# TransNormer attention and a squared-ReLU MLP: neighbouring tokens in a tile, one output transfer for two tiles, and a new order in the opening

## The chip, the cores and the metric

The kernel runs on one core of one Trainium2 chip. The metric is the device time of a launch in microseconds. A core has a matrix engine (TensorE, PE in the profile; its weight loads are PEld), three engines for elementwise work (VectorE or DVE, ScalarE or ACT, GpSimd or POOL) and SyncE (SP), which here only issues transfers. Sixteen DMA engines move the data.

## The reference

The inputs are `q`, `k`, `v` of (8 batches, 8 heads, 576 tokens, 64 features), and two weights that arrive as float64.

```
kv  = einsum('bhsd,bhse->bhde', k, v)
out = einsum('bhsd,bhde->bhse', q, kv)
x   = out / sqrt(mean(out*out, -1) + 1e-6) * g_norm      # per head
x   -> (4608 tokens, 512)
y   = (relu(x @ w_in) ** 2) @ w_out                      # 512 -> 2048 -> 512
```

## The kernel before

**Tiles and strips.** A batch has 576 tokens: four tiles of 128 (`C = 4`) and a rest of 64. The rests of two batches make one tile, so two batches give nine tiles (`PAIR = 9`) and there are 36. Four tiles are a strip of 512 tokens (`NT = 4`), and the main loop (L1171) runs over nine strips `s`. Each strip has an up part (x times `w_in`) and a down part (times `w_out`). From strip 1 on, both are done by recursive products of seven instead of eight blocks, so sums and differences of blocks fall to VectorE, GpSimd and ScalarE.

**Which tokens make a tile.** For batches 0 and 1 (`Q_ON_PE = 2`) the queries are transposed on TensorE (L384), and tile `c` holds the tokens `4*sp + c`. For batches 2 to 7 VectorE transposes them in blocks of 32 by 32 (L368). Their loads (L121) put token `16*i + k` of a batch in partition `i`, place `k`, with `i` below 32 and `k` below 16, in pieces of 32 features (128 bytes). After the transpose, tile `c` holds the tokens `16*i + 4*c + k`, so that its 128 rows lie in four groups. `out_rows` (L673) gives the rows of an output tile; for these batches it makes one transfer for each tile, with a destination of 4 groups by 32 rows. `send` (L824) is called for two tiles and half of the output columns at a time and issues them on SP; only in the last strip may the second go to ScalarE's queue.

**The weights.** They come as pairs of 32-bit words. `convert_on_act` (`act` in the list below) makes two ScalarE instructions for a piece of 128x512 (L242, L245), and `conversion` (`piece`) four VectorE instructions (L254, L256, L260, L263). There are 32 pieces; the first four are spread over the opening and the rest over the up part of strip 0, whose loads wait for a free one of 8 `raw` buffers. In the down part of strip 0 VectorE also makes the sums of the output weights (L280, `w_t`) that later strips stream from HBM as `w_blk`.

**The order.** Everything is issued in an order written out by hand: an engine takes its own instructions in that order. The attention is a list `slices`, of which `attend` runs a part after each product. In the opening, for a pair of heads `p`: `T` transposes queries (TensorE L384, copied by ScalarE L386), `K` makes keys times values (TensorE L408, copied by ScalarE L411 and L412, with the rest tokens from `k_rest` and `v_rest`), `Q` multiplies (L520) and squares (ScalarE L451) and takes means (VectorE L459), `N` normalizes (root on ScalarE, VectorE L470 to L474, L527), `F` transposes the features (L544, copied by ScalarE L545), and `U` is the first group of up products (L555), which needs the feature copy and the converted weight piece `p`.

**PSUM.** `apsum` has two rings: tag `at` with two buffers of one bank, for transposes and keys, and tag `x` with one buffer of two banks, for the products of queries (`products_x`, L429). `rest_queries` (L389) transposes the last queries of batches 0 and 1; its tile has tag `x`. In `slices` it follows `query_means` and `roots_normalized` of a pair of tiles, which write and read the tile `x_ps` of the same tag (L634 to L637).

**The start of the transfers.** SP issues query, key and value loads of the first pair of heads, then `load_rest(0, ...)` (two transfers for the rest tokens of keys and values), then the next pairs, with pieces of the weights between them. ScalarE's own queue issues two small loads of `g_norm`.

Of the kernel before, what the change touches and what calls it, by code (L numbers as in the profile page):

```python
# [10 lines left out]
FP32 = mybir.dt.float32  # L11
# [9 lines left out]
def kernel(  # L21
# [34 lines left out]
    nc = tc.nc  # L56
    P = 128
    B, H, S, D = q.shape
# [5 lines left out]
    C = S // P  # L64
# [10 lines left out]
    SQ = 32  # L75
    Q_ON_PE = 2
# [20 lines left out]
    apsum = opening.enter_context(tc.tile_pool(name="opsum", bufs=2, space=bass.MemoryType.PSUM))  # L97
# [5 lines left out]
    def load(b, p, q_eng, names="kvq", parts=range(4)):  # L103
        hs = slice(2 * p, 2 * p + 2)
        inputs = (("q", q, q_eng), ("k", k, nc.sync), ("v", v, nc.sync))
        if b == 0 and p >= 2:

            h_place = g_pool.tile([P, 4, C * P], FP32, name="first_qkv", tag="gt")
        if b == 1 and p == 2:
            h_place = spare_pool.tile([P, 3, C * P], FP32, name="more_qkv")  # L110
        placed = (b, p) in ((0, 2), (0, 3), (1, 2))
        for i, (n, src, eng) in enumerate(inputs if b == 0 else inputs[1:] + inputs[:1]):
            if n not in names:
                continue
            whole = src[b, hs, 0 : C * P].rearrange("h (sp c) d -> sp h c d", c=C)
            if n == "q" and b >= Q_ON_PE:

                t = qkv_pool.tile([P, 4 * C, SQ], FP32, name=n, tag=n, bufs=3) if 0 in parts else main[n, b, p]
                for a in parts:
                    h, f = divmod(a * SQ, D)  # L120
                    eng.dma_start(  # L121
                        out=t[ts(a, SQ)],
                        in_=src[b, 2 * p + h, 0 : C * P, f : f + SQ].rearrange("(i k) f -> i k f", k=4 * C),
                    )
            elif n != "q":
                if placed:
                    t = h_place[:, i].rearrange("p (h c d) -> p h c d", h=2, c=C)
                else:
                    t = qkv_pool.tile([P, 2, C, D], FP32, name=n, tag=n)
                eng.dma_start(out=t, in_=whole)  # L130
            else:

                if placed:
                    t = h_place[:, i].rearrange("p (c h d) -> p c h d", h=2, c=C)
                else:
                    t = qkv_pool.tile([P, C, 2, D], FP32, name=n, tag=n, bufs=3)
                for h in range(2):
                    eng.dma_start(out=t[:, :, h, :], in_=whole[:, h])
            main[n, b, p] = t
# [9 lines left out]
    def load_rest(b, eng):  # L149
        h = b % 2  # L150
        half = slice(REST * h, REST * (h + 1))
        for t, src in ((k_rest[half], k), (v_rest[half], v)):
            eng.dma_start(out=t, in_=src[b, :, C * P : S].rearrange("h s d -> s h d"))
# [20 lines left out]
    def load_next(q_eng=nc.sync, names="kvq"):  # L174
        u = next(to_load, None)
        if u is not None:
            load(*u, q_eng, names)
# [21 lines left out]
    def drip_queries():  # L199
        u = next(later_queries, None)  # L200
        if u is not None:
            drips.extend((load, (*u, nc.sync, "q", (2 * h, 2 * h + 1))) for h in range(2))
# [130 lines left out]
    nc.scalar.sqrt(one, one)  # L333

    load_next()
    load_rest(0, nc.sync)
    for p in range(1, NP):
        load_next()
        load_piece()
# [10 lines left out]
    def open_rest(b):  # L350
        t = qt_pool.tile([P, NP, P], FP32, name="qT_rest", tag="qT_rest", bufs=1)
        for p in range(NP):
            qT["rest", b // 2, p] = t[:, p]
        return t
# [32 lines left out]
        if (b, p) == (1, NP - 1):  # L387
            drip_queries()
    def rest_queries(b):  # L389
        ps = apsum.tile([P, 2, C, P], FP32, name="tr_ps", tag="x", bufs=1)[:, 0]  # L390
        for p in range(NP):
            nc.tensor.transpose(ps[:, p], flat(q_rest[b // 2][:, 2 * p : 2 * p + 2]), ident)
        nc.scalar.copy(open_rest(b), ps)
# [209 lines left out]
    def sums_x(s):  # L603
# [9 lines left out]
    slices, ready = [], {}  # L613

    act, T, K, Q, N, F, piece = (
        convert_on_act, transposed_query, key_value, first_queries, first_normalized, first_features, first_piece
    )
    U = first_up
    slices += [(T, (0, 0)), (K, (0, 0)), (Q, (0,)), (act, (0,))]
    slices += [(T, (0, 1)), (K, (0, 1)), (piece, (0, 2)), (N, (0,)), (Q, (1,)), (act, (1,)), (piece, (0, 2))]  # L620
    slices += [(T, (0, 2)), (K, (0, 2)), (piece, (1, 2)), (N, (1,)), (Q, (2,)), (F, (0,)), (act, (2,)), (piece, (1, 2))]
    slices += [(T, (0, 3)), (K, (0, 3)), (U, (0, [0])), (piece, (2, 2)), (N, (2,)), (Q, (3,)), (F, (1,)), (U, (0, [1, 2]))]
    slices += [(piece, (2, 1)), (N, (3,)), (act, (3,)), (F, (2,)), (U, (1, [0])), (piece, (2, 1)), (piece, (3, 4)), (F, (3,))]
    slices += [(U, (1, [1, 2])), (U, (2, [0, 1, 2])), (U, (3, [0, 1, 2]))]
    ready[0] = len(slices)
    def query_pairs(b):
        first_n = b // 2 * PAIR + (C if b % 2 else 0)
        ns = list(range(first_n, first_n + C + b % 2))
        return [ns[i : i + 2] for i in range(0, len(ns), 2)]
# [3 lines left out]
    for pair in query_pairs(1)[1::-1]:  # L633
        slices += [(query_means, (pair,)), (roots_normalized, (pair,))]  # L634
        if pair == query_pairs(1)[1]:
            slices.append((rest_queries, (1,)))
        slices += [(features, (n,)) for n in pair]  # L637
    ready[1] = len(slices)
    T, K, last = transposed_query, key_value, query_pairs(1)[2]
    slices += [(query_means, (last,)), (K, (2, 0, 1)), (T, (2, 0)), (roots_normalized, (last,)), (T, (2, 1))]  # L640
    slices += [(features, (last[0],)), (T, (2, 2)), (T, (2, 3)), (K, (2, 2, 3))]
    for b in range(2, B):
        pairs = query_pairs(b)
        for i, pair in enumerate(pairs):
            left = len(pairs) - i
            more = b + 1 < B
            at = left + (b == 2)
# [25 lines left out]
    def out_rows(n):  # L673

        to = []
        for t in range(2):
            m, c = divmod(n + t, PAIR)
            b, c_b = (2 * m, c) if c < C else (2 * m + 1, c - C - 1)
            if c == C:
                for h in range(2):  # L680
                    rows = out[(2 * m + h) * S + C * P : (2 * m + h + 1) * S, :]
                    to.append((slice(REST * h, REST * (h + 1)), slice(t, t + 1), rows.rearrange("p (t e) -> p t e", t=1)))
                continue
            if t and c_b > 0:
                continue
            cs = slice(c_b, c_b + (1 if t or c_b == C - 1 else 2))
            both = slice(t, t + cs.stop - cs.start)
            rows = out[b * S : b * S + C * P, :]
            if b < Q_ON_PE:
                to.append((slice(0, P), both, rows.rearrange("(sp c) e -> sp c e", c=C)[:, cs]))  # L690
            else:
                rows = rows.rearrange("(i c k) e -> k i c e", c=C, k=4)
                to += [(slice(0, P), slice(t + j, t + j + 1), rows[:, :, c]) for j, c in enumerate(range(cs.start, cs.stop))]
        return to


# [127 lines left out]
    def send(s, th, eh, o):  # L824
        for i, (part, t, rows) in enumerate(out_rows(NT * s + 2 * th)):
            eng = nc.scalar if i % 2 and s == N_STRIP - 1 and (th, eh) == (0, 1) else nc.sync
            eng.dma_start(out=rows[:, :, ts(eh, DH)], in_=o[part, t, :])
# [339 lines left out]
    apsum = psums.enter_context(tc.tile_pool(name="apsum", bufs=2, space=bass.MemoryType.PSUM))  # L1167
# [3 lines left out]
    for s in range(N_STRIP):  # L1171
        attend(ready[s])
        if s == DEEP_UP - 1:
# [4 lines left out]
            apsum = ctx.enter_context(tc.tile_pool(name="apsum", bufs=1, space=bass.MemoryType.PSUM, reuse_waits="tile"))  # L1178
# [16 lines left out]
        for i, (w, fn, a) in enumerate(steps):  # L1195
# [28 lines left out]
            if s:  # L1224
                clock[0] += 3.2 if i >= n_up else 2.2 if s == DEEP else 1.2
                soon = tiles_due and tiles_due[0][2][0] // NT == s + 1
                if i == n_up + 10:
                    while tiles_due and tiles_due[0][2][0] // NT == s + 1:
                        _, f, a = tiles_due.popleft()
# [62 lines left out]
```

## Time and profile before

| | |
|---|---|
| median of 3 runs | 922.79 us (921.88 to 923.62) |
| the profiled execution | 923.58 us; its span 921.5 us |
| TensorE matmul busy | 889.9 us, 97% of the span |
| weight loads, VectorE, ScalarE, GpSimd busy | 829.1, 730.1, 318.6, 305.7 us |
| DMA moved | 235.71 MB, mean 256 GB/s; the SP queue's packets took 79.5% of 16 engines' time |
| mean granted TensorE clock | 0.987 |

The span is from the first to the last event of the trace; about 2 us of the execution lie outside it. The profile has times from the start of the span. A busy time is the union of an engine's instructions. A number in brackets in the timeline is the time in which the engine was idle before the instruction, with what ended the wait. "SPq" and "ACTq" are the queues of SyncE and ScalarE that issue transfers. L numbers are lines of the kernel before.

### The profile page before, as it was taken

To read this page: it belongs to the slowest core of one execution; us is meant where nothing else is said; L and a number is where in the kernel's file an instruction comes from. 1 tells how busy PE (TensorE), PEld (TensorE's weight loads), DVE (VectorE), ACT (ScalarE), POOL (GpSimd) and SP (SyncE) were. 2 spreads that over 40 slices of the span, in tenths; PEclk is the share of its full clock that TensorE was granted. 3 is DMA by queue.
4 is the path that set the end of the run, shared out by engine and by line. 5 is a ranking of instruction groups with operands and counts; after the bars stand their busy time and mean duration, and the time that the engine had idled before them with its cause. 6 is when DMAs were issued, how large, how long until landed. Compare 5 with 4: busy or idle time off the path is not lost.

```text
span 921.5 us, 20643 instructions
## 1 busy us (share of the span) xinstructions
PE 889.9 (97%) x8246; PEld 829.1 (90%) x8246; DVE 730.1 (79%) x1256; ACT 318.6 (35%) x638; POOL 305.7 (33%) x315
## 2 busy tenths in 40 slices
PE   7999799999999999999999999999999999999996
PEld 6534588789999999999999999999999999999996
DVE  3899959568968895889688966986789768976885
ACT  3797323321024601370137012710272027102800
POOL 0000000910157504650465044704361437145700
PEclk8999899999999999999999999999999999999999
DMA  9599998798979697989777978888657865784484
GB/s 282 203 297 298 302 360 249 214 279 309 307 247 245 236 326 244 238 263 329 251 219 240 326 262 214 246 296 299 197 176 270 293 189 187 287 289 156 155 304 147
DMA packets 172079, 235.71 MB, mean 256 GB/s; under 512 B 83280, under 2 KB 137040, under 8 KB 163536
## 3 DMA queue, kind: packets, MB, share of 16 engines
q1 hardware_dynamic: 171692, 234.27, 79.5%
q8 instruction: 65, 1.06, 0.5%
q14 instruction: 30, 0.25, 0.1%
q10 hardware_dynamic: 292, 0.13, 0.0%
HBM read 197.66 MB, written 36.70 MB: 254 GB/s over the span
## 4 chain that ended last, share of the span: by engine, by line
PE 79%; DMA 8%; DVE 7%; issue 2%; SPq 2%; ACT 2%; DVEq 0%; ACTq 0%
PE ps_B L933 20%; PE ps_A L1121 16%; PE ps_A L933 15%; PE ps_B L1121 8%; PE ps_A L712 5%; PE ps_C L1121 4%; PE ps_B L712 3%; PE kv_ps L408 2%; DMA w_blk<-w_deep 2%; PE x_ps L442 2%; PE ps_C L712 1%; DVE w_c L260 1%; DMA xT<-x_d 1%; DMA w_blk<-w_out 1%; DMA raw<-in_moe_w_out_dram 1%
## 5 line engine op out<-in xcount | busy, mean ns | idle before, releaser
L933 PE MATMUL ps_B<-w_blk,g_s 128*128 128x128 f32 x1024 | 126.2, 275 | 0.0
L933 PEld LDWEIGHTS ps_B<-w_blk,g_s 128*128 128x128 f32 x1024 | 120.0, 192 | 0.2
L1121 PE MATMUL ps_A<-x_l,w_in 128*128 128x128 f32 x784 | 104.2, 276 | 1.1 <-ACT snap L1138 1.1
L280 POOL TENSOR_TENSOR x_l<-xT 128x256 f32<-128x256 f32 x21 | 16.1, 768 | 249.6 <-PE ps_A L933 249.6
L933 PE MATMUL ps_B<-w_blk,gt 128*128 128x128 f32 x768 | 97.5, 275 | 0.3 <-DMA w_blk<-w_out 0.3
L1121 PEld LDWEIGHTS ps_A<-x_l,w_in 128*128 128x128 f32 x784 | 95.4, 192 | 1.8 <-ACT snap L1138 1.3
L933 PE MATMUL ps_A<-w_blk,g_s 128*128 128x128 f32 x768 | 93.6, 275 | 0.0
L933 PEld LDWEIGHTS ps_B<-w_blk,gt 128*128 128x128 f32 x768 | 91.5, 192 | 0.7 <-issue 0.5
L933 PEld LDWEIGHTS ps_A<-w_blk,g_s 128*128 128x128 f32 x768 | 89.6, 192 | 0.0
L1133 POOL TENSOR_TENSOR snap<-snap,gt 128x512 f32<-128x512 f32 x35 | 46.6, 1332 | 124.3 <-ACT snap L1138 71.3
L1138 ACT COPY snap<-ps_A 128x512 f32<-128x512 f32 x63 | 36.7, 582 | 133.3 <-PE ps_A L1121 121.8
L948 DVE TENSOR_TENSOR o_sb<-o_sb,ps_B 128x256 f32<-128x256 f32 (+1 forms) x128 | 49.5, 387 | 35.0 <-ACT o_sb L949 27.6
L1071 ACT ACTIVATE gt<-gt 128x512 f32<-128x512 f32 x112 | 69.7, 622 | 18.1 <-DVE gt L1133 18.0
L933 PE MATMUL ps_A<-w_blk,gt 128*128 128x128 f32 x576 | 72.3, 275 | 1.3 <-DMA w_blk<-w_deep 1.3
L1072 ACT ACTIVATE gt<-gt 128x512 f32<-128x512 f32 x112 | 70.6, 631 | 3.6
L933 PEld LDWEIGHTS ps_A<-w_blk,gt 128*128 128x128 f32 x576 | 68.2, 192 | 1.5 <-DMA w_blk<-w_deep 1.5
L1031 POOL TENSOR_TENSOR w_i<-w_in 128x512 f32<-128x512 f32 x7 | 8.9, 1268 | 157.0 <-DVE w_in L280 157.0
L1133 POOL TENSOR_TENSOR gt<-gt,snap 128x512 f32<-128x512 f32 x42 | 52.6, 1279 | 24.9 <-DVE snap L1133 24.8
L280 DVE TENSOR_TENSOR gt<-gt 128x2048 f32<-128x2048 f32 (+1 forms) x29 | 59.7, 2063 | 0.0
L949 ACT COPY o_sb<-ps_A 128x128 f32<-128x128 f32 x24 | 6.4, 266 | 147.3 <-PE ps_A L933 147.3
L1121 PE MATMUL ps_A<-x_l,w_blk 128*128 128x128 f32 x392 | 52.3, 276 | 1.4 <-issue 1.2
L1121 PE MATMUL ps_B<-x_l,w_blk 128*128 128x128 f32 x392 | 52.0, 276 | 0.0
(174 smaller groups left out, 1823.9 us busy)
## 6 DMA issues: line engine op xcount, KB each, us to landing
w_blk<-w_deep SPq DMA_DIRECT2D x56, 1024.0 KB
w_blk<-w_out SPq DMA_DIRECT2D x56, 768.0 KB
w_blk<-w_in_deep SPq DMA_DIRECT2D x49, 768.0 KB
raw<-in_moe_w_in_dram SPq DMA_DIRECT2D x16, 512.0 KB
raw<-in_moe_w_out_dram SPq DMA_DIRECT2D x16, 512.0 KB
k<-in_k_dram SPq DMA_DIRECT2D x29, 256.0 KB
v<-in_v_dram SPq DMA_DIRECT2D x29, 256.0 KB
x_d<-x_q SPq DMA_DIRECT2D x27, 256.0 KB
```

Source lines behind the costliest of these rows:

```text
L260: yield nc.vector.scalar_tensor_tensor(out=ci, in0=high, scalar=-(2**30), in1=ci, op0=ALU.bitwise_and, op1=ALU.bitwise_or)
L280: eng.tensor_tensor(out=out, in0=a, in1=b, op=ALU.subtract)
L408: nc.tensor.matmul(ps[ts(h, D), i], lhsT=a, rhs=w, start=c == 0, stop=c == C)
L442: nc.tensor.matmul(ps[half, r, i, ts(p, D)], lhsT=q[row, half], rhs=kvd[b, p][row, row], start=True, stop=True)
L712: nc.tensor.matmul(bank[BANK[p]][:, i, :], lhsT=lhsT(k), rhs=rhs(k), start=p in (1, 5, 2) and i == 0 and k == 0, stop=k == n - 1, skip_gro ...
L933: nc.tensor.matmul(chain[c][x][:, i, :], lhsT=a[:, f, :], rhs=w[:, f, :], start=x not in opened[c] and f == 0, stop=f == FQ // 2 - 1, skip ...
L948: add = lambda out, a, b: nc.vector.tensor_tensor(out=out, in0=a, in1=b, op=ALU.add)
L1071: nc.scalar.activation(o, o, AF.Relu)
L1072: nc.scalar.activation(o, o, AF.Square)
L1121: nc.tensor.matmul(ps[:, i, :], lhsT=w, rhs=rhs, start=j in (1, 2, 5) and i == 0, stop=True, skip_group_check=True)
L1133: add = lambda eng, out, a, b: eng.tensor_tensor(out=out, in0=a, in1=b, op=ALU.add)
L1138: nc.scalar.copy(t, ps)
```

## The change

Five edits. The loads of the queries of batches 2 to 7 put token `32*k + i` in partition `i`, place `k`, so a tile is 128 neighbouring tokens; `out_rows` then gives one transfer of (128 rows, 2 tiles, 256 columns) where it gave two of (4, 32, 256). `load_rest(0)` goes from SP's queue to ScalarE's. `rest_queries` takes its PSUM tile from tag `at`. The opening's list puts each `act` behind the next pair's `K` copies and `Q`, and `F` and the pieces where shown. In strip 1's list `T (2, 2)` changes places with a `features`.

```diff
-   in_=src[b, 2 * p + h, 0 : C * P, f : f + SQ].rearrange("(i k) f -> i k f", k=4 * C),
+   in_=src[b, 2 * p + h, 0 : C * P, f : f + SQ].rearrange("(k i) f -> i k f", k=4 * C),
...
-    load_rest(0, nc.sync)
+    load_rest(0, nc.scalar)
...
-        ps = apsum.tile([P, 2, C, P], FP32, name="tr_ps", tag="x", bufs=1)[:, 0]
+        ps = apsum.tile([P, C, P], FP32, name="tr_ps", tag="at")
...
-    slices += [(T, (0, 0)), (K, (0, 0)), (Q, (0,)), (act, (0,))]
-    slices += [(T, (0, 1)), (K, (0, 1)), (piece, (0, 2)), (N, (0,)), (Q, (1,)), (act, (1,)), (piece, (0, 2))]
-    slices += [(T, (0, 2)), (K, (0, 2)), (piece, (1, 2)), (N, (1,)), (Q, (2,)), (F, (0,)), (act, (2,)), (piece, (1, 2))]
-    slices += [(T, (0, 3)), (K, (0, 3)), (U, (0, [0])), (piece, (2, 2)), (N, (2,)), (Q, (3,)), (F, (1,)), (U, (0, [1, 2]))]
-    slices += [(piece, (2, 1)), (N, (3,)), (act, (3,)), (F, (2,)), (U, (1, [0])), (piece, (2, 1)), (piece, (3, 4)), (F, (3,))]
+    slices += [(T, (0, 0)), (K, (0, 0)), (Q, (0,)), (T, (0, 1)), (K, (0, 1)), (N, (0,)), (Q, (1,)), (act, (0,))]
+    slices += [(T, (0, 2)), (F, (0,)), (K, (0, 2)), (piece, (0, 2)), (N, (1,)), (Q, (2,)), (act, (1,)), (piece, (0, 2))]
+    slices += [(T, (0, 3)), (F, (1,)), (K, (0, 3)), (U, (0, [0])), (piece, (1, 2)), (N, (2,)), (Q, (3,)), (act, (2,))]
+    slices += [(piece, (1, 2)), (U, (0, [1, 2])), (piece, (2, 1)), (N, (3,)), (act, (3,)), (F, (2,)), (U, (1, [0]))]
+    slices += [(piece, (2, 3)), (F, (3,)), (piece, (3, 4))]
...
-    slices += [(features, (last[0],)), (T, (2, 2)), (T, (2, 3)), (K, (2, 2, 3))]
+    slices += [(T, (2, 2)), (features, (last[0],)), (T, (2, 3)), (K, (2, 2, 3))]
...
-            rows = out[b * S : b * S + C * P, :]
-            if b < Q_ON_PE:
-                to.append((slice(0, P), both, rows.rearrange("(sp c) e -> sp c e", c=C)[:, cs]))
-            else:
-                rows = rows.rearrange("(i c k) e -> k i c e", c=C, k=4)
-                to += [(slice(0, P), slice(t + j, t + j + 1), rows[:, :, c]) for j, c in enumerate(range(cs.start, cs.stop))]
+            rows = out[b * S : b * S + C * P, :].rearrange("(sp c) e -> sp c e" if b < Q_ON_PE else "(c sp) e -> sp c e", c=C)
+            to.append((slice(0, P), both, rows[:, cs]))
```

## The prediction

> **What bounds the kernel now.** I read the page's busy times, then the slices, the waits of TensorE, and the timeline where TensorE waits.
>
> ```profile
> PE 889.9 (97%) x8246; PEld 829.1 (90%) x8246; DVE 730.1 (79%) x1256; ACT 318.6 (35%) x638; POOL 305.7 (33%) x315
> PE   7999799999999999999999999999999999999996
> DMA  9599998798979697989777978888657865784484
> ```
>
> ```profile
> PE tr_ps L392 <- DVE x_n L510: 6.4, 1, 6.4
> PE x_ps L520 <- ACT kv_all L412: 4.5, 3, 3.3
> PE xt_ps L570 <- DVE x_n L510: 1.7, 1, 1.7
> PE ps_A L1121 <- ACT snap L1138: 1.1, 1, 1.1
> ```
>
> TensorE is the bound: 31.6 us of the span (921.5 less 889.9) are without a matmul. The digits are tenths in 40 slices of 23 us: the idle time sits in the first, the fifth and the last, and in few waits: what can be gained is these waits and their consequences.
>
> ```profile
> 11.70 0.33 PE L408 MATMUL kv_ps<-v_rest,k_rest 64*64 64x64 f32 x4
> ...
> 13.30 0.66 ACT L242 ACTIVATE w_c<-raw 128x512 f32<-128x512 f32 x1 [1.95 <-DMA raw<-in_moe_w_in_dram]
> ...
> 13.87 0.66 ACT L245 ACTIVATE raw<-raw 128x512 int32<-128x512 uint32 x1
> ...
> 14.42 0.57 ACT L386 COPY qT<-t_ps 128x512 f32<-128x512 f32 x1
> ...
> 15.37 2.08 PE L520 MATMUL x_ps<-kv_all,qT 128*128 128x128 f32 x8 [3.34 <-ACT kv_all L412]
> ```
>
> Opening: ScalarE stands at a weight piece that lands at 13.28. The copies behind it had their matmuls done at about 12.0; TensorE waits 3.34 us.
>
> ```profile
> 60.00:70.00 10.00, 10.00 (x24) 4.30 (x23) 10.00 (x21) 9.78 (x24) 0.00 (x0) 0.91 1.07 296
> ...
> 100.00:110.00 10.00, 5.84 (x102) 4.69 (x100) 9.87 (x18) 2.31 (x6) 0.00 (x0) 0.98 1.05 326
> 110.00:120.00 10.00, 7.79 (x29) 6.71 (x30) 6.98 (x14) 0.59 (x1) 0.00 (x0) 0.68 1.02 327
> ```
>
> ```profile
> 110.70 1.29 DVE L510 TENSOR_TENSOR x_n<-x_ps,newton 128x512 f32<-128x512 f32 x2
> ...
> 112.21 1.08 PE L392 MATMUL tr_ps<-ident,q_rest 128*128 128x128 f32 x4 [6.37 <-DVE x_n L510]
> ...
> 113.08 5.29 PE L712 MATMUL ps_C<-w_in,gt 128*128 128x256 f32 x16
> ...
> 118.21 3.62 PE L712 MATMUL ps_B<-w_in,g_s 128*128 128x256 f32 x16
> ```
>
> The first three rows are windows of 10 us: PE, weight loads, DVE, ACT, POOL, granted clock, DMA share, GB/s. From 40 to 112 us VectorE is full with conversions and sums, and TensorE and ScalarE nearly so. At 105.8 TensorE comes to the last queries and waits for their bank until VectorE's x_n has read it, 6.37 us; then the clock is low (0.68).
>
> ```profile
> ACT snap L1138 <- DMA out_dram<-o_sb: 2.9, 1, 2.9
> ```
>
> ```profile
> 914.82 0.42 DVE L948 TENSOR_TENSOR o_sb<-o_sb,ps_B 128x256 f32<-128x256 f32 x1
> 915.32 1.32 ACTq L827 DMA_DIRECT2D out_dram<-o_sb  x1
> ```
>
> Output: one transfer held a buffer until TensorE waited (at 749), and the end is a DMA: the last VectorE instruction ends at 915.24, the span at 921.5.
>
> **What the skill says.** (1) "DMA: Bandwidth & Descriptors", section on why a DMA increments its semaphore by 16: a transfer is spread over the largest number of engines, up to 16, that divides the slowest dimension on both sides. For (4, 32, 256) that is 4, for (128, 2, 256) it is 16. The trace agrees: the 48 output transfers of the first form have 5 semaphore updates each (4 engines, and the rest at once), the others 16. From issue to landing they take 3.3 to 8.0 us, with 2.4 to 6.6 us between first and last update; the six (128, 2) ones have 0.2 to 1.3 us there. (2) "TensorE: Matmul & The Clock Gate", Part 1: the clock is halved after about 3.4 us of idleness. The trace agrees and is sharper: half clock at 14.0 to 24.3 and 109.6 to 116.5, after both waits, and at 58.4 to 61.8 after a wait of only 2.01 us. (3) The DMA page, "Issuing engines are not separate DMA queues": another issuer saves issue time only. Here that is 0.65 + 0.64 us on SP.
>
> **The change part by part**, against the profiled 923.58 us (span 921.5 and 2.1 around it).
>
> *Opening order.* The same instructions, permuted. I laid the three queues out in order with the durations of the timeline (L242 0.57 us apart, L245 0.55, copies 0.22 and 0.47, squares 0.5, the four conversion steps 0.4, 0.42, 0.62, 0.62, products 0.97 or at half clock 1.87) and the landings of the trace. In the old order this gives 36.9 for the end of the first group's first tile, which the trace has at 36.74. In the new order the second pair's key copies end at 12.4 (15.3 before), its product at 13.6 (17.5). `act 0` comes at 14.1, so piece 0 ends at 21.2, not 20.3, and piece 1 at 26.1 (25.3). The fourth features come at 29.5 (32.3), piece 3 at 32.0 (33.8), the tile at 34.0. With the half clock of before it would be 36.7, with one slow window 34.8. The following conversions on VectorE, which wait for ScalarE behind this tile, begin 0.2 to 2.9 us earlier. As VectorE is then full to 112, all moves with it. The loads of pieces follow the freeing of buffers and the DMA is only 0.44 busy at 30 to 40, so they follow.
>
> *Rest loads on ScalarE.* Two issues of 0.65 us leave SP; later loads go out up to 1.3 us earlier. On ScalarE's queue they stand after the table load and before the two g_norm issues; its first work is at 6.24, so nothing waits. The first keys' product waited 0.61 us for `v_rest` (landed 8.46), which goes; the DMA at 1.04 takes part back. Worth 0.7. Both opening edits together: 0.2 to 3.8, I take **3.0**.
>
> *Last queries in tag `at`.* No instruction more. TensorE no longer waits for x_n, but for `q_rest`: issued 101.88, landed 106.7, when TensorE was there at 105.8. So 0.9 us stay, of 6.37. Behind the transposes stand ps_C x16 and ps_B x16, whose inputs are there (g_s ends at 102.2); they run while VectorE still works. The clock stays up: ps_C takes 3.45 instead of 5.08 and the transposes 0.6 instead of 1.08, 2.1 us. The features behind them need x_n of 112.0 less the 3.0, due after the products at about 111: covered. ScalarE's copy (0.59) meets an idle engine; the ring's earlier user was copied at 101.7. Gain 5.5 + 2.1, less 0.3 for a product that may still meet a slow window: **7.3**, between 5 (the wait alone, with a later `q_rest`) and 8.5.
>
> *What is late next:* the streamed `w_blk` in strip 0. TensorE comes to the first at about 116 (127.2 before); it landed at 117.05, less 3.0. The third landed at 132.2 and is wanted at 131. DMA is at 1.0 from 60 to 130, so 3.0 is all that it moves, and the margin is 2 us. Strips 0 and 1 also have the DMA at 0.92 to 0.97 from 180 to 260. I take **2.4 back** here.
>
> *T before features in strip 1.* VectorE's order stays; the features of 172.55, which wait 1.68 us for x_n, come one step (1.73 us of TensorE) later. **1.5**, between 0 and 1.7.
>
> *Output.* 48 transfers of 128 KB on 4 engines become 30 on 16: 18 of two tiles, and 12 of one tile where its neighbour is of another batch or a rest. SP saves 17 issues of 0.57 us. The wait at 749 goes (1.1), and transfers behind them land 1 to 3 us earlier: at 658 and 667, where 0.85 and 0.27 are waited after xT landings. **1.5**, between 0 and 2. At the end the two last landed at 919.5 and 920.7, issued 915.27 and 915.32. One transfer of 256 KB has 3.63 us at the least here beside other traffic, and 128 KB on 16 engines 1.94; I take 2.7, landing 918.0: **2.6**.
>
> *Query loads.* Also 512 packets of 128 bytes, now 8 KB apart in a partition rather than 256 bytes. The trace doesn't show that pattern[...]. From both sides: 10% less, or twice the 14 ns that such packets take now. The 49,152 of them are 43 us of each DMA engine over 560 us that have some 70 us free. I take nothing.
>
> Sum 3.0 + 7.3 + 1.5 + 1.5 + 2.6 - 2.4 = 13.5, so 910.1. The median of the runs is 0.8 below the profiled one: **909.3**.
>
> **The rivals.** (A) As summed: 0.62, 905 to 914. For it: each wait has its named releaser. (B) The DMA's backlog takes the middle: TensorE comes early to `w_blk` at 116 to 140 and waits there, so of the 7.3 only the clock's and little else stays. For it: latencies of 10 to 12 us there; against: queues were empty at 133. Then 15.9 less 8 or 9: 915; 0.18. (C) The opening stays at half clock and B holds too, so that the end and the outputs alone remain: 919; 0.09, and nearly half of it within 0.2%. (D) Slower: query packets at 8 KB cost more. The DMA takes 43 us for them in stretches that have 70 free; from three times the price (42 ns) on, the 86 more take that and the gains, and TensorE waits for xT and `w_blk`. At 3.4 times: 103 - 70 - 16, some 17 worse, about 940. For it: nothing shows the pattern; against: the rest's queries, loaded by 128 bytes from four heads, land in 1.7 us at best. 0.07. (E) That it doesn't do what it says: the transfers stay split, as the two sides' shapes differ. Then 4 less is gained: 913; 0.04.
>
> A measurement of this kernel tells about 0.2%, 1.9 us, from no change. Faster 0.89 (A, B, E and half of C), same 0.04, slower 0.07. The range leaves out D and the ends: 904.5 to 918.5.
>
> **What would show it.** The product of L520 behind the second keys starts near 12.5; no wait over 1.5 us before tr_ps; a clock of 1.0 at 110 to 120; no wait of TensorE at L570 in strip 1 or behind an output; 16 updates in every tall output transfer and under 4 us from the last VectorE instruction to the span's end. Wrong if TensorE waits for `w_blk` between 110 and 145 by more than 3 us, if the clock is low after 14 us, or if 128-byte packets take over 20 ns.

## The result, and the profile after

The kernel after takes 919.11 us in the median (911.88 to 922.25), the kernel before in the same sitting 923.99: a ratio of 0.9936, interval 0.9911 to 0.9961. The ratio is an estimate from all runs, not the quotient of the two medians, which would be 0.9947. The medians of the kernel before went from 923.99 to 926.72 between sittings and chips, so each kernel below has its ratio to runs of the kernel before on the same chip, and these ratios are compared; a hundredth is 9.2 us. The change gains 5.9 us (3.6 to 8.2), where 13.5 were forecast. One of its ten runs, 911.88, is 4 us under all others, so what holds the kernel back is not the same in every execution; that run has no trace. The profiled execution took 920.21 us, its span 918.0. In its lines all numbers from L687 on are 4 lower.

The page's busy times, and its slices of TensorE and DMA:

```profile
PE 888.5 (97%) x8246; PEld 825.8 (90%) x8246; DVE 731.3 (80%) x1256; ACT 318.3 (35%) x638; POOL 305.8 (33%) x315
...
PE   7899998999999999999999999999999999999998
...
DMA  9699898898989697979886987888657866785385
```

TensorE still has 29.5 us without a matmul (31.6 before). The idle slice has moved: it was the fifth (92 to 115 us), now it is the seventh (138 to 161). The list of TensorE's waits says what stands there:

```profile
PE ps_A L708 <- DVE o_sb L878: 3.3, 1, 3.3
PE x_ps L520 <- ACT kv_all L412: 2.1, 3, 0.9
...
PE xt_ps L570 <- DVE x_n L510: 1.4, 2, 1.0
```

The wait of 6.4 us for x_n is gone, and so is that for an output at 749. At the top is a wait that was in no list before: a product waits for an output sum on VectorE. The timeline of the kernel after, in order of time (what ended the wait stands in brackets):

```profile
105.99 0.69 DVE L280 TENSOR_TENSOR w_t<-w_in 128x512 f32<-128x512 f32 x1 [3.89 <-DMA w_out<-wt]
...
106.83 0.63 PE L392 MATMUL tr_ps<-ident,q_rest 128*128 128x128 f32 x4 [1.04 <-DMA q_rest<-in_q_dram]
107.30 3.62 PE L708 MATMUL ps_C<-w_in,gt 128*128 128x256 f32 x16
...
115.38 1.32 PE L570 MATMUL xt_ps<-ident,x_n 128*128 128x128 f32 x8 [1.01 <-DVE x_n L510]
...
137.38 7.17 PE L708 MATMUL ps_B<-w_blk,gt 128*128 128x256 f32 x32 [0.88 <-DMA w_blk<-w_out]
...
140.68 1.29 DVE L280 TENSOR_TENSOR w_in<-w_in 128x512 f32<-128x512 f32 x2 [8.01 <-DMA w_out<-w_in]
...
147.08 0.68 DVE L878 TENSOR_TENSOR o_sb<-ps_A,snap 128x512 f32<-128x512 f32 x1
...
147.82 8.80 PE L708 MATMUL ps_A<-w_blk,gt 128*128 128x256 f32 x32 [3.27 <-DVE o_sb L878]
```

In the kernel before, the first of these lines was

```profile
102.06 0.69 DVE L280 TENSOR_TENSOR w_t<-w_in 128x512 f32<-128x512 f32 x1
```

Read the list from the top. VectorE's first deep sum `w_t` stands for 3.89 us at a store of `wt` to memory; before, it began at 102.06 without a wait. TensorE comes to tr_ps 5.4 us earlier than before and is 7.5 us ahead at the products behind it; at the features (L570) it waits 1.01 us for `x_n`, which VectorE now begins at 114.6 (110.7 before). But VectorE's sums feed SP's stores, and these the loads: the first `w_blk` lands at 121.1 (117.1 before), the fourth at 146.0 (141.1), and the stores of w_out that went out at 123.1 and 124.1 go out at 128.3 and 129.4 and land at 138.9 and 140.6. VectorE waits 8.01 us for these, since its next sums overwrite what they read. Behind those sums in VectorE's order stands the output sum of product 7, and for that sum's bank TensorE waits. The windows show the clock (last columns: PE clock, DMA share, GB/s):

```profile
100.00:110.00 10.00, 8.96 (x119) 7.58 (x118) 6.04 (x12) 2.08 (x5) 0.00 (x0) 1.00 0.64 187
110.00:120.00 10.00, 8.96 (x45) 7.27 (x43) 9.76 (x20) 1.86 (x4) 0.00 (x0) 1.00 0.99 294
140.00:150.00 10.00, 6.73 (x27) 5.47 (x26) 9.15 (x15) 0.00 (x0) 0.00 (x0) 0.89 0.84 274
```

The clock is full at 110 to 120, as forecast; the half clock has moved to the new wait (147.7 to 151.1). Of the 7.5 us nothing is left at 151. The end, from the timeline:

```profile
914.45 0.42 DVE L944 TENSOR_TENSOR o_sb<-o_sb,ps_B 128x256 f32<-128x256 f32 x1
914.94 0.37 SPq L823 DMA_DIRECT2D out_dram<-o_sb  x1
```

VectorE ends at 914.87, as before within 0.4; the span ends 3.1 us later instead of 6.3. That is nearly all that this execution gained.

In the opening, ScalarE's part of the timeline and the product named in the forecast:

```profile
6.36 1.63 ACTq L344 DMA_DIRECT2D g_col<-in_g_norm_dram  x2
...
8.04 0.58 ACT L386 COPY qT<-t_ps 128x512 f32<-128x512 f32 x1 [5.81 <-DMA k<-in_k_dram]
...
15.51 1.16 PE L520 MATMUL x_ps<-kv_all,qT 128*128 128x128 f32 x8 [0.52 <-ACT kv_all L412]
```

The product behind the second keys starts at 15.51 (15.37 before), not near 12.5. In the kernel before, the first two of these lines were

```profile
0.91 1.45 ACTq L344 DMA_DIRECT2D g_col<-in_g_norm_dram  x2
...
6.24 0.59 ACT L386 COPY qT<-t_ps 128x512 f32<-128x512 f32 x1 [4.00 <-PE t_ps L384]
```

The g_norm issues, at 0.91 before, now stand in ScalarE's queue until 6.36, and the first copy behind them comes at 8.04. In the trace, the semaphore that tells of the landing of each g_norm load is one that an earlier load on SP also has, and the issue goes out when that load has landed: the first at 6.36, behind queries that landed at 6.34, the second at 7.50, behind keys that landed at 7.48.

### The profile page after: what moved, and what is told of

Read it like the earlier page. It is cut to its first block, busy times and chain, and to the rows that moved or that the text cites. A ratio compares the mean times of both kernels' runs of the same rounds, so it can differ in the third digit from the quotient of the medians.

```text
span 918.0 us, 20609 instructions
## 1 busy us (share of the span) xinstructions
PE 888.5 (97%) x8246; PEld 825.8 (90%) x8246; DVE 731.3 (80%) x1256; ACT 318.3 (35%) x638; POOL 305.8 (33%) x315
## 3 DMA queue, kind: packets, MB, share of 16 engines
HBM read 197.66 MB, written 36.70 MB: 255 GB/s over the span
## 4 chain that ended last, share of the span: by engine, by line
PE 72%; DVE 11%; DMA 9%; ACT 3%; issue 2%; SPq 2%; DVEq 0%; ACTq 0%
PE ps_B L929 20%; PE ps_A L1117 16%; PE ps_A L929 15%; PE ps_B L1117 8%; PE ps_C L1117 4%; PE ps_A L708 4%; DMA q<-in_q_dram 2%; PE kv_ps L408 2%; PE x_ps L442 1%; PE ps_B L708 1%; DMA w_out<-w_in 1%; DMA w_blk<-w_out 1%; DVE w_c L260 1%; DVE w_t L280 1%; DVE o_sb L944 1%
```

## The experiments

Two questions: where the lead of the middle went, and where the opening's 3.0 us stayed. **Theory M** (place): the streamed tiles lie over the buffers of the raw weight pieces. In the compiled programs, each of the two opening edits by itself gives these buffers other addresses. In the kernel before, the first `w_t` lies over older pieces; in the kernel after, half of it lies over the very last one, so that VectorE must wait for its store. With one opening edit alone it would be the last but one; no run shows what that costs. Rival **B** is that of the prediction: the DMA is full, and TensorE would have to wait anyway. For the opening: **Q**, the rest loads on ScalarE's queue spoil a good order; **O**, the order itself gains nothing.

| kernel | median, us | ratio to before | interval |
|---|---|---|---|
| after | 919.11 | 0.9936 | 0.9911 to 0.9961 |
| e1_old_place | 914.08 | 0.9874 | 0.9853 to 0.9895 |
| e2_rest_on_sp | 911.74 | 0.9859 | 0.9838 to 0.9880 |
| e3_g_norm_first | 913.27 | 0.9870 | 0.9850 to 0.9891 |
| e4_old_opening | 911.09 | 0.9853 | 0.9835 to 0.9870 |
| e5_queries_alone | 920.95 | 0.9955 | 0.9935 to 0.9976 |
| e6_output_alone | 918.86 | 0.9929 | 0.9905 to 0.9952 |
| e7_swap_alone | 923.61 | 0.9984 | 0.9968 to 1.0000 |
| e8_wait_put_in | 917.52 | 0.9918 | 0.9892 to 0.9944 |
| e9_q_rest_one_earlier | 911.94 | 0.9865 | 0.9839 to 0.9892 |
| e10_q_rest_two_earlier | 914.22 | 0.9884 | 0.9860 to 0.9907 |
| e11_sums_later_after | 917.81 | 0.9889 | 0.9843 to 0.9935 |
| e12_best | 911.90 | 0.9847 | 0.9807 to 0.9887 |
| e13_early_loads_new | 912.66 | 0.9858 | 0.9824 to 0.9893 |
| e14_early_loads_old | 911.54 | 0.9852 | 0.9814 to 0.9889 |

TensorE's lead: the start of the same matmul after less before, in us, from the two traces. The columns are the matmul's time in the kernel before; the fourth lies in the product after tr_ps, the sixth in the product for which the kernel after waits at 147.8 (it begins at about 148.7 in the kernel before). A minus is a lead. Each trace is one execution, so differences of less than 1 or 2 us between traces say little; those of e1, e5 and e9 are of their fastest run, those of e6 and e11 of their slowest.

| kernel | 31 | 60 | 96 | 116 | 142 | 151 | 175 | 749 |
|---|---|---|---|---|---|---|---|---|
| after | -0.1 | -0.5 | 0.0 | -7.5 | -4.7 | +0.6 | -0.6 | -0.3 |
| e1 | -1.6 | -2.2 | +0.8 | -6.3 | -6.3 | -5.6 | -6.5 | -9.9 |
| e2 | -0.2 | -0.8 | +1.2 | -6.1 | -6.1 | -5.1 | -6.0 | -8.1 |
| e4 | 0.0 | -0.1 | +0.4 | -6.9 | -6.9 | -6.3 | -7.2 | -9.2 |
| e5 | -0.5 | -1.1 | -0.4 | -7.6 | -7.6 | -7.6 | -5.2 | -6.5 |
| e8 | +0.5 | +0.6 | +2.3 | -5.2 | -3.3 | 0.0 | -0.9 | -3.1 |
| e9 | -1.7 | -2.2 | -2.3 | -11.0 | -11.0 | -8.2 | -9.1 | -10.9 |
| e12 | -1.1 | -0.8 | -1.0 | -9.6 | -9.0 | -4.7 | -5.5 | -7.7 |

**e1: a place over older pieces for w_t.** Added to the kernel after, where the stream's pool is opened; `stream()` takes this tile for its first block:

```diff
+                first_block.append(stream_pool.tile([P, 4, FQ // 2, P], FP32, name="w_blk", tag="w_blk"))
+                nc.gpsimd.memset(first_block[0][:, 0, 0, 0:1], 0.0)
```

> The kernel after with one thing more: the first streamed block's tile is written once by GpSimd (one element per partition) before the first deep sum takes its tile, so that the deep sum's tile w_t lies over buffers of older weight pieces, as it did in the kernel before, and the block's own over the last ones. Theory M (place): the first w_t instruction starts at about 102.1 instead of 105.99, the store of w_deep at 104.7 instead of 108.6, the first w_blk lands near 117 instead of 121; VectorE's wait of 8.0 us at 140.7 falls under 3 us, TensorE's 3.3 us behind o_sb goes; 914 to 916 us. Rival B (the DMA queues are full, so the landings don't follow): w_blk lands at 121, 127 and 137 as before, TensorE waits for it; 918 to 920 us.

Its timeline:

```profile
102.92 0.68 DVE L280 TENSOR_TENSOR w_t<-w_in 128x512 f32<-128x512 f32 x1
...
107.97 0.63 PE L392 MATMUL tr_ps<-ident,q_rest 128*128 128x128 f32 x4 [1.28 <-DMA q_rest<-in_q_dram]
...
115.34 1.04 PE L570 MATMUL xt_ps<-ident,x_n 128*128 128x128 f32 x8
...
136.06 1.29 DVE L280 TENSOR_TENSOR w_in<-w_in 128x512 f32<-128x512 f32 x2 [4.06 <-DMA w_out<-w_in]
...
143.20 7.17 PE L708 MATMUL ps_A<-w_blk,gt 128*128 128x256 f32 x32 [0.41 <-DVE o_sb L882]
```

The wait is gone, the first `w_blk` lands at 117.7, VectorE's second wait is 4.06 instead of 8.01 (under 3 was expected), and of TensorE's 3.27 us 0.41 are left. A write of one column, which the load then overwrites, is worth 5.7 us (0.9874 against 0.9936). Theory M holds, and B fails at this size.

**e8: the same wait put into a kernel that hasn't it.** The base is e4, the kernel after with the opening of before:

```diff
         t = deep.pop(p)
+        if p == 1:
+            nc.vector.memset(deep[2][:, 0, 0, 0:1], 0.0)
         deep_sums([t[:, i] for i in range(4)], w)
```

`deep[2]` is here reserved ahead, with GpSimd's writes of one column into three other tiles of the pool, so that it lies over the last pieces.

> e4_old_opening with one instruction more on VectorE ahead of the first w_t: a write of one element per partition into the tile of the second deep sum, which lies over the last weight pieces and so waits for the same stores that w_t waits for in the kernel after (three such writes on GpSimd fix the places of the tiles). Theory M: VectorE stops there for 3 to 4 us until about 106, the wait for stores of w_out grows to about 8 us, TensorE waits about 3 us for o_sb; 4 to 5.5 us slower than e4_old_opening, 915 to 917. Rival (the opening's order is what costs the kernel after its 5 us): 911 to 912.

Its timeline:

```profile
108.33 0.06 DVE L841 MEMSET w_t<- 128x1 f32 x1 [3.88 <-DMA w_out<-wt]
...
141.68 1.29 DVE L280 TENSOR_TENSOR w_in<-w_in 128x512 f32<-128x512 f32 x2 [6.58 <-DMA w_out<-w_in]
...
148.82 6.53 PE L708 MATMUL ps_A<-w_blk,gt 128*128 128x256 f32 x29 [2.98 <-DVE o_sb L884]
```

In e4 the first `w_t` has no wait:

```profile
102.50 0.69 DVE L280 TENSOR_TENSOR w_t<-w_in 128x512 f32<-128x512 f32 x1
```

A write of 0.06 us brings the whole chain back, with the old opening: 0.9918 against e4's 0.9853, 6.0 us by the runs, a little over the 4 to 5.5 expected. Its trace is 2.3 us late at 96 already; TensorE's lead there goes from 5.2 at 116 to nothing at 151. So the opening's edits cost the kernel after its time through the place of `w_t`.

**e2, e3, e4: the opening.** e2 is e1 with the first of these edits, e3 is e1 with the second (and the g_norm lines taken out below). e4 is the kernel after with the order of the opening and the rest loads as before, and without e1's write.

```diff
-    load_rest(0, nc.scalar)
+    load_rest(0, nc.sync)
```

```diff
     load_next()
+    g_col = const.tile([P, 1], FP32, name="g_col")
+    g_src = g_norm.rearrange("(d u) -> d u", u=1)
+    for h in range(2):
+        nc.scalar.dma_start(out=g_col[ts(h, D)], in_=g_src)
     load_rest(0, nc.scalar)
```

> As e1_old_place, with the two loads of the first keys' rest back on SP's queue. Theory Q (two more loads ahead of the two g_norm loads on ScalarE's queue hold ScalarE's first copy and take the first tiles' bandwidth): the two g_norm issues go back to about 0.9 us, the first qT copy starts near 6.2 instead of 8.04, the first relu at 33 to 35 instead of 36.7; 1.5 to 3.5 us less than e1_old_place. Rival O (the new order itself gains nothing): first relu at 36.3 to 37, time within 1 us of e1_old_place.

> As e1_old_place, with the two g_norm loads issued ahead of the two rest loads on ScalarE's queue, so that they meet free semaphores. If theory Q's wait in the queue is the cause: the g_norm issues at 0.9 to 2.2, the first qT copy behind its matmul at 7.0 to 7.2 (the first queries land at 6.3, as bandwidth is shared), first relu at 34 to 35.5. If the shared bandwidth of the first 8 us is the cause: qT copy at 7.0 or later and first relu at 36 to 37 all the same. Rival O: 36.3 to 37.

> The kernel after with both opening edits undone (order and queue of the rest loads); the buffers of the weight pieces then lie as in the kernel before, without the extra write. Theory M with O: VectorE's first w_t at 102.1 without a wait; TensorE's lead of about 7 us at 116 falls to no less than 3 by 150; 912 to 915 us. Rival (the opening order is worth its 3 us, hidden by the rest): 3 us slower than e1_old_place.

ScalarE in e3:

```profile
0.91 1.44 ACTq L339 DMA_DIRECT2D g_col<-in_g_norm_dram  x2
...
5.37 0.59 ACT L385 COPY qT<-t_ps 128x512 f32<-128x512 f32 x1 [3.14 <-PE t_ps L383]
```

The hold in the queue is as theory Q says: the issues are back at 0.91, the first copy 2.7 us earlier than in the kernel after (7.0 to 7.2 were expected). In e2 it is at 6.04. Yet the first relu comes at 36.62 in e3, 36.55 in e2, 36.80 in e4: theory O. In e1 it came at 35.13; that lead of 1.6 to 2.2 us was lost by 79, where TensorE waited 3.1 us for queries. The new order is worth nothing that the runs can tell (0.9859 against 0.9853, each within 0.002). The loads on ScalarE's queue cost 1.4 us by the ratios (e1 against e2), but the intervals overlap and e1's trace is the one ahead at 31, so a cost of theirs is not shown. e4, without any of the opening, is the best of these: 13.6 us (12.0 to 15.3).

**e5, e6, e7: the other parts alone,** each on the kernel before, with the lines of the change as they stand in its diff: e5 the PSUM tile of `tr_ps`, e6 the query loads and `out_rows`, e7 the swap in strip 1.

> The kernel before with the last queries' transposes in the ring at and nothing else. The prediction's terms: 7.3 for the wait and the clock, 2.4 handed back at w_blk, so 4.9 less. What e4_old_opening shows (lead of 6.9 us at 116, 6.4 left at 149): 6 to 7 us less than before, 917 to 918. Rival B (transfers take it): under 2 us.

> The kernel before with the query loads and output rows of 128 neighbouring tokens and nothing else. The prediction's terms 1.5 and 2.6: 4.1 less. What e4_old_opening shows (1.6 us of TensorE between 625 and 749, end 3.1 shorter): 4.5 to 5 us less, 919 to 920; if the query loads cost anything, less than 4.

> The kernel before with the one swap of strip 1 (queries' transposes of key pair 2 ahead of the features) and nothing else. Prediction: 1.5 less. What e4_old_opening shows at that place (a wait of 0.78 us instead of 1.68): 0.9 less. Rival: taken again by the next wait, 0.

The queries bring 4.2 us (2.2 to 6.0) by the runs, under the 6 to 7 expected; the trace gains more up to 151 (7.6) and loses 2.4 to x_n in strip 1, the wait that the swap is for. The output brings 6.6 (4.4 to 8.8), more than expected; its trace shows 3.1 at the end, and TensorE no earlier (1.5 us come at 749 and 1.6 go at 621, where TensorE waits for a streamed block). That trace is of its slowest run, 920.49; what more the others have is not found in it. The swap: 1.5 (0 to 3.0), not clear of nothing by the runs; in its trace the wait at L570 in strip 1 is gone, and TensorE gains 1.7 us between 151 and 175. The three sum to 12.3, and e4, which has just these, has 13.6; within these intervals no part is seen to take from another.

**e9, e10: earlier q_rest.** e4 with step 14 (e9) or 13 (e10):

```diff
-                if i == 15:
+                if i == 14:
                     for b in range(2):
                         load_q_rest(b, nc.sync)
```

> e4_old_opening with the loads of the last queries' q_rest issued one step of strip 0's first products earlier (step 14 instead of 15), so ahead of the last stores of wt on SP's queue. If the wait of 1.2 us for q_rest is what is left of the prediction's term: q_rest lands 2 to 4 us earlier, the wait ahead of tr_ps goes to under 0.3 us, 0.5 to 1.2 us less than e4_old_opening, 910 to 910.6. Rival: the transfers there are taken in order and the last pieces or stores land later by the same, or the next wait takes it: 911 to 912.

> As e9_q_rest_one_earlier, two steps earlier (step 13). The same gain as there if the wait is all that counts, 910 to 910.6; if the loads now come ahead of keys or weight pieces that are wanted sooner, TensorE waits in front of the transposes at 96 by 1 us more: 911.5 to 912.5.

TensorE's waits in e9's timeline, with the transposes now without one:

```profile
103.33 0.60 PE L392 MATMUL tr_ps<-ident,q_rest 128*128 128x128 f32 x4
...
140.63 7.17 PE L708 MATMUL ps_A<-w_blk,gt 128*128 128x256 f32 x32 [2.51 <-DVE o_sb L878]
```

The wait goes, TensorE is 11.0 us ahead, and 2.5 of it are lost at 140.6: the next wait takes it, and the time can't be told from e4's. In e10 TensorE waits 1.25 us at 98.8 in front of other transposes, as expected of loads that come too early.

**e11, e12: the sums that stand ahead of that output sum, later.** In the kernel after (e11) and in e9 (e12):

```diff
-            if i - n_up in (7, 8, 9, 12):
+            if i - n_up in (9, 10, 11, 12):
```

> The kernel after with the first two of strip 0's four sums of the up weights placed behind two later products (steps 9, 10, 11, 12 instead of 7, 8, 9, 12), so that VectorE meets the wait for the stores of w_out behind the output sums of product 7, not ahead of them. VectorE's late first w_t (105.99) stays. Theory: the lead of TensorE is lost at 147.8 because that output sum stands behind these sums in VectorE's order; then its wait of 3.3 us and the half clock behind it go, 913.5 to 915.5. Rival: VectorE is too late by then whatever the order, or the wait comes back at the next output sum: 917 to 919.5.

> e9_q_rest_one_earlier (old opening, earlier q_rest) with the same move of the sums. If the wait for o_sb at 140.6 (2.5 us) was what took its gain: under 0.5 us there and 908.5 to 910; if later waits take it (w_deep at 242, x_n at 165): 911 to 912.

The same place in e11's timeline:

```profile
140.24 7.17 PE L708 MATMUL ps_B<-w_blk,gt 128*128 128x256 f32 x32 [0.71 <-DMA w_blk<-w_out]
...
151.15 8.83 PE L708 MATMUL ps_A<-w_blk,gt 128*128 128x256 f32 x32 [3.74 <-DMA w_blk<-w_out]
```

I had expected the wait to go. It only changes its releaser: the block that the same product needs lands at 151.0, in e12 at 142.4 with a wait of 2.37. Two chains, by the output sum and by the streamed block, end here within 2 us of each other (the block landed at 146.0 and the sum ended at 147.8 in the kernel after, 138.7 and 140.6 in e9). That both begin at VectorE's deep sums is read from the traces, not tested by itself. This much of rival B is right: of the kernels with the new place for the last queries, those without VectorE's extra wait begin this product at 140.6 to 143.7 (e10 at 146.4), those with it at 147.8 to 151.2, and of the 4.7 us by which e9 leads e1 at 116, 2.6 are left here. A version faster than e4 wasn't found; e12's interval holds e4's ratio.

**e13, e14: who takes the opening's lead.** The next batch's loads four steps of strip 0 earlier, in e1 and in e4:

```diff
-                if i in (4, 6, 8):
+                if i in (0, 2, 4):
                     load_next()
-                if i == 5:
+                if i == 3:
```

> e1_old_place (new opening, w_t in the old place) with the loads of the next batch's first three key pairs issued four steps of strip 0 earlier (steps 0, 2, 4 instead of 4, 6, 8, the rest's at 3 instead of 5), in the stretch 37 to 60 where the DMA share is 0.7 to 0.9. If transfers between 60 and 93 are what took the lead of the opening (1.6 to 2.2 us at 31 to 60 in e1_old_place): no wait of TensorE over 1 us between 70 and 100, the lead against before stays at 1.5 to 2.5 us up to 97, tr_ps at 105 to 106.5, 1.5 to 2.5 us less than e1_old_place. Rival (VectorE's conversions set the end of this stretch whatever the transfers do): tr_ps at 107.5 to 108.5, time within 1 us.

> e4_old_opening with the same earlier loads: the control. Its VectorE had no wait before 93.9, so if the transfers only bound a kernel that is ahead, it gains 0 to 0.8 us: 910.3 to 911.1, and e13_early_loads_new is 1 to 2 us under it. Rival (as above, or the opening leads by nothing in most executions): e13 within 1 us of this one or above it.

Neither gains beyond the intervals (e13's ratio is 1.5 us under e1's and level with e14's). TensorE's wait at 58 grew from 2.0 to 3.7 and 4.5 us, as ScalarE had to wait for raw pieces there, and the one at 79 (3.1 us in e1) went to 0.6 and to nothing; at 96 both are about half a us behind the kernel before. e14, with the old opening, leads by 2.1 at 31 in its trace and loses it; e9, with the old opening as well, leads by 1.7 and keeps it. So a lead at 31 comes and goes between executions with either order, and isn't always kept. One thing that goes with it is the clock: before the first relu TensorE is at half clock for one, two or three stretches of 3.41 us, whatever the order (in e13 none is on record). With one, the first relu comes at 35.13 in the new order (e1) and at 34.71 and 35.99 in the old (e14, e7); with two, at 36.55 to 36.70 in the new (after, e2, e3) and at 35.10 to 36.28 in the old (e9, e12, e6); with three, at 36.59 in the new (e11) and at 36.27 to 38.07 in the old. With as many slow stretches, the new order isn't clearly the earlier one in these traces. Whether transfers or VectorE's chain of conversions take a lead after 31 is left open by these runs.

## Why the prediction was wrong

**Opening, 3.0: measured as nothing, and this step failed first.** The schedule by hand kept the landings of before. Two more loads on ScalarE's queue moved them: the first queries landed at 6.34 (4.98), v at 8.43 (6.65), and the g_norm issues held the first copy. But e2, with the loads back on SP, gains nothing against e4 either, so the order itself was over-rated.

The term that was off is the start of `act 0`: 14.1 was worked out, 17.07 is what e2 has and 17.20 the kernel after (13.30 before). It stands behind the second pair's copies and product, and in e2 these key copies end at 14.4, not 12.4, and the product at 16.5, not 13.6: TensorE was at half clock from 11.0 to 17.8, past the 14 of the signs, and `v_rest` landed at 9.12 (8.46 before). Behind `act 0` the schedule was right: from its start to the first relu it is 19.5 us in every trace of the new order, where 19.9 were worked out and the kernel before has 23.5. So the new order saves 4.0 us behind `act 0` and begins it 3.8 us later.

The prediction's own figures for a slow clock, 34.8 with one slow window and 36.7 with the half clock of before, are near to what came: 35.13 with one (e1), 36.55 to 36.70 with two or three (e2, e3, after, e11). But its 3.0 counts on one slow window at most, and so sets the new order with a fast clock against the old one with a slow clock. "All moves with it" doesn't hold either: e1's lead of 2.2 at 60 was gone at 79.

**w_blk, "117.05, less 3.0": it landed at 121.1.** This step took the landings of the middle as the old ones or better. It left out that an edit in the opening can give the raw buffers other addresses, and so give `w_t` a wait of 3.9 us that is in no line of the profile before; this is the largest single error. That is worth 5.7 us (e1 against after) or 6.0 (e8 against e4). The forecast of 2.4 handed back was for another reason, and in e4, without this wait, about 0.5 is handed back (6.9 at 116, 6.3 at 151).

**Last queries, 7.3: right at its place.** In e4 the lead goes from +0.4 at 96 to -6.9 at 116; the wait left at tr_ps is 1.04 in the kernel after, 0.9 forecast. By itself (e5) the edit is worth 4.2 in the time, since 2.4 of it go to `x_n` in strip 1.

**Swap, 1.5: what the runs say, with an error as large** (0 to 3.0); the wait at L570 fell from 1.68 to 0.44 in the kernel after, 0.78 in e4.

**Output, 1.5 and 2.6: right at the end (3.1).** All 72 output transfers now have 16 updates, as the Trainium skill has it ("DMA: Bandwidth & Descriptors", section on why a DMA increments its semaphore by 16). In the middle the wait at 749 (1.1) is gone; those at 658 and 667 stand as before (0.84 and 0.27 in the kernel after), and between 600 and 752 TensorE gains 2.2 in e4, 0.9 in the kernel after and nothing in e6. **Query loads, nothing: right.** The 128-byte packets behind 100 us, nearly all of them the query loads', took 14.0 ns in the mean before and 13.7 in the kernel after. **Rest loads on ScalarE, 0.7 of the 3.0: not seen.** By the ratios they cost 1.4, which the intervals leave open. The same page of the Trainium skill, section "Issuing engines are not separate DMA queues", says that another issuer saves issue time alone. That much came (SP's first load of the second pair goes out at 3.33, at 4.71 before); I counted what SP saved and not what stood behind the issues on ScalarE's queue, where "nothing waits" was wrong: the first copy came 1.8 us later.

Two readings of the profile in the prediction don't hold, though the sum doesn't rest on them. ScalarE isn't nearly full to 112: it is busy for 6.3 and 6.8 us in the windows from 80 to 100 and for 2.3 in the next. And the traces don't agree with a clock that halves after 3.4 us of idleness: the half clock at 14.06 set in 2.0 us after the wait began, and the one at 58.43 followed a wait of 2.01.

Put together by the runs' ratios: queries, output and swap bring 13.6 (e4), the new order -0.6, the rest loads -1.4, the place of `w_t` -5.7, which makes the 5.9 measured. These are steps from one kernel to the next (e4, e2, e1, after), so they close by themselves; the check from outside is e8, with 6.0 for the place of `w_t`. That e4 comes to the 13.5 of the forecast is luck: it lacks the 3.0 of the opening. Without the opening the forecast was 10.5 (7.3, 1.5, 1.5 and 2.6, less 2.4). Of the 3.1 that e4 has more, by the traces 1.9 are what was not handed back at `w_blk` and 0.5 the end; the rest is not located. Rival B, with 915 and a wait at `w_blk`, came nearer in time, and it names the right stretch; but the transfers were late there since VectorE was, not by a backlog of their own. Rival C names the time, 919, but by luck: in it the opening stays slow, as it did, but a backlog takes the middle and the outputs alone remain, where e1 and e4 show that one wait on VectorE took it.

## What to carry to other kernels

When an edit changes when or in which order buffers are first taken, look at what the later pools' tiles lie over: a wait for a tile's last reader can come into being far from the edit, and no line of the old profile has it. A forecast that keeps old landings must ask, for every chain behind an edited one, what issues each transfer and what that waits for. And a lead of the bounding engine is worth only as much as the next supply chain lets through: here two chains end at the same product within 2 us, and when one was moved the wait came from the other.

## What was not expected

The issue of a DMA can stand in a compute engine's queue: the two g_norm issues came at 0.91 us where they were the first on ScalarE, and at 6.36 where the two rest loads stood ahead of them, and ScalarE's first copy came behind them (8.04 in the kernel after, 5.37 in e3). And the opening differs between executions by more than its edits were worth: with the same old order TensorE was between 2.1 us ahead (e14) and 1.3 behind (e10) at 31 us, with one window of half clock in the first and three in the second.
